# Dense 512-column matmuls added before every second key transpose job, and between the last value chunks, of a decode attention kernel

## The chip, the cores and the metric

The kernel runs on one core of one Trainium2 chip. The metric is the device time of one execution in microseconds (us). The four executions of the kernel before beside the result lie within 0.23% (448.83 to 449.87); eleven beside the experiments within 0.5 to 0.65% (447.58 to 450.48 at the widest). A single profiled execution reports a "span", from its first to its last instruction, which in these runs is 1.7 to 3.2 us shorter than the time (median 1.8). HBM is the chip's main memory, PSUM the memory that matmuls write to, in banks.

PE is the matmul engine (TensorE), PEld its weight loads, DVE the vector engine, ACT the scalar engine, POOL GpSimd, SP the engine that issues most transfers. The "granted clock" is the share of PE's full clock that the profile says was granted: in every stretch of these traces 1.00 or 0.50, and between the two only as the mean of a window with a switch in it.

## The reference, cut to what matters

Two independent decode attention blocks (one query token, batch 4, 32 query heads, 8 key/value heads, head size 128, 8192 cached positions) are computed and put side by side. Block A attends to all 8192 positions, block B to the last 2048.

```python
def _A_ref(x, k_cache, v_cache, wq, wo):          # B: the same on k_cache[:, :, Sk - W:, :]
    q = (x @ wq).reshape(B, Sq, Hq, Dh).transpose(0, 2, 1, 3)
    k = jnp.repeat(k_cache, rep, axis=1)
    v = jnp.repeat(v_cache, rep, axis=1)
    scores = jnp.einsum("bhqd,bhkd->bhqk", q, k) * (Dh ** -0.5)
    p = _softmax(scores, axis=-1)
    o = jnp.einsum("bhqk,bhkd->bhqd", p, v)
    return o.transpose(0, 2, 1, 3).reshape(B, Sq, Hq * Dh) @ wo
```

Each key and value is used by four query heads only. There is little arithmetic per byte: about 185 MB have to come in from HBM, and all of it once (184.56 MB read in the profile before).

## The kernel before

The work is cut into 40 units: 8 of block B, then 32 of block A, one for each key/value head and batch entry. A unit of block A loads 2 MB of keys and 2 MB of values. Keys arrive with positions on the partitions, so PE transposes them first: 8 jobs ("T") a unit, each of 4 transposes into a PSUM bank, which DVE (even jobs) or ACT (odd jobs) copies out. Then come score matmuls ("S", 8 columns wide), and the value matmuls ("PV", 4 columns wide) of the unit before, in four chunks of 16. PE's order within a unit is

```python
TOKENS = [("T", 0), ("T", 1), ("OT",), ("T", 2), ("T", 3), ("S", 0), ("S", 1), ("X",),
          ("T", 4), ("T", 5), ("S", 2), ("S", 3), ("PV", 0), ("PV", 1), ("OL",),
          ("T", 6), ("T", 7), ("S", 4), ("S", 5), ("PV", 2), ("PV", 3), ("S", 6), ("S", 7), ("OPJ",)]
```

OT, OL and OPJ occur in every fourth unit only (13, 17, ... 37): there the finished heads of four units are rearranged and multiplied with the output weights, four matmuls of 512 columns. The transpose job:

```python
def pe_T(u, k):
    ...
    bkf = bank_f(KTB[jobs[idx]["bank"]])
    def fn(pe):
        ins = None
        for pi in range(4):
            t0 = k * 8 + 2 * pi
            ins = pe.transpose(out=bkf[:, pi * 128:(pi + 1) * 128],
                               in_=K_sbf[:, slot, t0:t0 + 2, :].rearrange("p t d -> p (t d)"),
                               identity=identf[:, :])
        return ins
    op("pe", fn, waits=[("K", u) if k == 0 else None, bankfree(idx), ("setup",)], inc=("T", idx))
```

Keys and values each have four buffers. A key transfer is issued once the last transpose job of the unit four before it is done; a value transfer once the value work four units before is done:

```python
def sp_K(u):
    waits = [("T", tjob_idx[(u - NKS, NB - 1)])] if u >= NKS else []
    ...
def sp_V(u):
    waits = [("PV", (u - NVS) * NQ + NQ - 1)] if u >= NVS else []
    ...
```

Units 10 to 37 (LB0 to LB1 - 1) run as seven turns of a loop on PE, four units a turn, and all turns have the same instructions. Units 38 and 39 (L = 39 is the last) follow outside. Unit 38 has no value work in it; unit 39 does that of unit 37. The end of the program does what is left:

```python
for c in range(NQ):
    pe_PV(L - 1, c)
add(dve_norm(L - 1))
for c in range(NQ):
    pe_PV(L, c)
add(dve_norm(L))
pe_OPJ(L // Bn)          # the last projection: 8 matmuls of 256 columns
```

## Time and profile before

449.64 us, median of three runs (448.83 to 449.87). The profiled execution has a span of 447.8 us.

| what | value | seen in |
|---|---|---|
| DMA engines, mean busy share, 10 us windows from 20 to 430 us | 0.95 to 1.07 | windows |
| rate there from 220 us on | 421 to 432 GB/s | windows |
| PE busy | 83% | busy times |
| mean granted clock | 0.797 | cores |
| transposes of one pair of jobs (8 instructions) | 1.97 us at clock 0.50, 0.93 to 1.09 at 1.00 | timeline |

These lines of the page's 40 slices show the tenths of granted PE clock and of DMA busy share, and the rate:

```profile
PEclk9996569989886899866596689867875986788596
DMA  8999999999999999999999999999999999999991
GB/s 337 411 415 438 413 421 415 420 421 423 423 422 421 425 422 425 424 429 427 427 427 430 430 424 426 430 428 427 429 426 427 426 430 429 426 424 430 430 403 65
```

Transfers fill the program from end to end (a DMA share of 1.01 and 425 GB/s on average from 20 to 430 us) while the PE clock swings (0.50 to 1.00 in the same windows of 10 us).

PE matters where the transfers run out. Its timeline at the end of the program (start in us, duration, engine, line, operation, output <- inputs, shape, count; in brackets the idle time just before and what ended it; L332 = transposes, L371 = scores, L397 = values, L483 and L474 = projections):

```profile
411.14 1.09 PE L332 MATMUL ps<-identf,K_sb 128*128 128x128 f32 x8 [0.79 <-DMA K_sb<-in_A_k_cache_dram]
412.68 0.27 PE L416 MATMUL ps<-ident,OTg 128*16 128x128 bf16 x1 [0.44 <-DVE KT_sb L340]
413.35 1.97 PE L332 MATMUL ps<-identf,K_sb 128*128 128x128 f32 x8 [0.41 <-ACT KT_sb L341]
...
422.51 1.86 PE L483 MATMUL ps<-W,OL 128*4 128x512 bf16 x4
...
424.83 2.69 PE L332 MATMUL ps<-identf,K_sb 128*128 128x128 f32 x16
...
431.81 2.08 PE L332 MATMUL ps<-identf,K_sb 128*128 128x128 f32 x16
...
438.96 0.39 PE L397 MATMUL ps<-PT,V_sb 128*128 128x4 bf16 x10
440.17 3.31 PE L397 MATMUL ps<-PT,V_sb 128*128 128x4 bf16 x118 [0.82 <-issue]
443.79 1.86 PE L474 MATMUL ps<-W,OTg 128*4 128x256 bf16 x8 [0.31 <-DVE OTg L592]
```

The keys of unit 37 land at 411.1 us and end PE's last wait for a key transfer. From there PE is busy nearly all the time until the last projection at 443.8 (30.19 of 32.65 us). The clock falls during unit 37, from 1.00 to 0.50 at 412.71 us: the first transpose pair takes 1.09 us, the next 1.97.

### The profile page before, as it was taken

Reading aid. Unit: us, or ns where it says so; the run is one execution under the profiler, and the core shown is the slowest. Engines: PE = TensorE matmul, PEld = TensorE weight load, DVE = VectorE, ACT = ScalarE, POOL = GpSimd, SP = SyncE. Lnnn points to the kernel's source line nnn. Section 1 sums busy time; section 2 is a strip of 40 time slices with the busy share of each in tenths; the row PEclk is TensorE's granted clock in tenths of the full one; section 3 lists DMA queues with packets and bytes.
Section 4 is the critical chain, followed back from the end, with each engine's and each line's share of the span. In section 5 each row is a group of like instructions: output and inputs, shape, how many; then the busy total and the mean of one; then the engine's idle time right before and its main releaser. Section 6 shows DMA issues by size and latency. Waiting matters only on the chain.

```text
span 447.8 us, 14767 instructions
## 1 busy us (share of the span) xinstructions
PE 373.4 (83%) x6783; PEld 339.4 (76%) x6783; DVE 195.9 (44%) x451; ACT 179.2 (40%) x202; POOL 40.1 (9%) x126
## 2 busy tenths in 40 slices
PE   0685199899676999988998998899889998988997
PEld 0685199768561898878898887879878987878896
DVE  0354055656440455434363444344443544344363
ACT  1163045435330464434264434334442543435261
POOL 1100000001100011000010001000110100010010
PEclk9996569989886899866596689867875986788596
DMA  8999999999999999999999999999999999999991
GB/s 337 411 415 438 413 421 415 420 421 423 423 422 421 425 422 425 424 429 427 427 427 430 430 424 426 430 428 427 429 426 427 426 430 429 426 424 430 430 403 65
DMA packets 17270, 185.01 MB, mean 413 GB/s; under 512 B 1860, under 2 KB 2392, under 8 KB 4824
## 3 DMA queue, kind: packets, MB, share of 16 engines
q1 hardware_dynamic: 15096, 178.27, 94.4%
q10 hardware_dynamic: 2080, 6.30, 3.5%
q8 instruction: 22, 0.36, 0.3%
q14 instruction: 8, 0.07, 0.0%
q0 software_dynamic: 64, 0.01, 0.0%
HBM read 184.56 MB, written 0.01 MB: 412 GB/s over the span
## 4 chain that ended last, share of the span: by engine, by line
DMA 54%; PE 35%; issue 4%; ACT 3%; DVE 2%; POOL 0%; ACTq 0%; POOLq 0%
DMA K_sb<-in_A_k_cache_dram 41%; PE ps L332 19%; DMA W<-in_A_wq_dram 7%; DMA W<-in_B_wo_dram 6%; PE ps L397 6%; PE ps L371 5%; PE ps L483 3%; ACT KT_sb L341 3%; PE ps L278 1%; DVE KT_sb L340 1%; DVE Dt L543 0%; DVE M L505 0%; ACT PT L554 0%; PE ps L474 0%; PE ps L438 0%
## 5 line engine op out<-in xcount | busy, mean ns | idle before, releaser
L341 ACT ACTIVATE KT_sb<-ps 128x1024 bf16<-128x1024 bf16 x160 | 163.0, 1023 | 244.9 <-PE ps L332 243.1
L332 PE MATMUL ps<-identf,K_sb 128*128 128x128 f32 x1280 | 217.1, 329 | 32.9 <-DMA K_sb<-in_A_k_cache_dram 17.5
L332 PEld LDWEIGHTS ps<-identf,K_sb 128*128 128x128 f32 x1280 | 179.0, 170 | 46.2 <-DMA K_sb<-in_A_k_cache_dram 18.6
L340 DVE COPY KT_sb<-ps 128x512 int32<-128x512 int32 x160 | 110.4, 690 | 138.9 <-PE ps L332 137.7
L397 PE MATMUL ps<-PT,V_sb 128*128 128x4 bf16 (+1 forms) x2560 | 76.2, 165 | 3.6 <-DMA V_sb<-in_A_v_cache_dram 1.8
L371 PEld LDWEIGHTS ps<-RQc,KT_sb 128*128 128x128 bf16 x2048 | 72.9, 100 | 4.5 <-ACT KT_sb L341 1.2
L371 PE MATMUL ps<-RQc,KT_sb 128*128 128x8 bf16 x2048 | 74.3, 167 | 0.9 <-ACT KT_sb L341 0.8
L397 PEld LDWEIGHTS ps<-PT,V_sb 128*128 128x128 bf16 x2560 | 70.8, 97 | 3.9 <-DMA V_sb<-in_A_v_cache_dram 2.0
L575 POOL PARTITION_ALL_REDUCE LB<-L x40 | 17.3, 432 | 155.2 <-DVE L L566 155.2
L514 POOL PARTITION_ALL_REDUCE MB<-M x32 | 11.9, 371 | 173.3 <-DVE M L505 173.3
L483 PE MATMUL ps<-W,OL 128*4 128x512 bf16 x60 | 22.5, 537 | 4.8 <-DMA W<-in_B_wo_dram 4.8
L592 DVE TENSOR_TENSOR OTg<-ps,RL 128x4 bf16<-128x4 f32 (+1 forms) x40 | 6.9, 173 | 40.2 <-PE ps L397 40.2
L505 DVE TENSOR_REDUCE M<-ps 128x4 f32<-128x256 f32 (+1 forms) x40 | 19.1, 477 | 10.8 <-PE ps L371 10.8
L566 DVE TENSOR_REDUCE L<-PT 128x4 f32<-128x256 bf16 (+1 forms) x40 | 21.9, 547 | 3.3 <-ACT PT L554 2.8
L371 PE MATMUL ps<-RQB,KT_sb 128*128 128x16 bf16 x512 | 18.6, 171 | 2.1 <-issue 1.2
L371 PEld LDWEIGHTS ps<-RQB,KT_sb 128*128 128x128 bf16 x512 | 17.9, 99 | 3.0 <-issue 1.5
L554 ACT ACTIVATE PT<-Dt 128x256 bf16<-128x256 f32 (+1 forms) x40 | 18.1, 452 | 4.0 <-DVE Dt L543 2.0
L483 PEld LDWEIGHTS ps<-W,OL 128*4 128x4 bf16 x60 | 5.6, 104 | 15.3 <-issue 8.7
L278 PE MATMUL ps<-xT,W 128*128 128x4 bf16 x256 | 7.4, 165 | 10.9 <-DMA W<-in_A_wq_dram 10.6
L278 PEld LDWEIGHTS ps<-xT,W 128*128 128x128 bf16 x256 | 7.0, 101 | 11.1 <-DMA W<-in_A_wq_dram 10.7
L543 DVE TENSOR_TENSOR Dt<-ps,MB 128x256 f32<-128x256 f32 x32 | 13.3, 415 | 0.5 <-POOL MB L514 0.5
L257 PE MATMUL ps<-ident,xo_sb 4*128 4x4 bf16 x8 | 0.6, 170 | 14.2 <-POOL identf L617 14.2
(49 smaller groups left out, 64.6 us busy)
## 6 DMA issues: line engine op xcount, KB each, us to landing
K_sb<-in_A_k_cache_dram SPq DMA_DIRECT2D x32, 2048.0 KB, 32.0
V_sb<-in_A_v_cache_dram SPq DMA_DIRECT2D x31, 2048.0 KB, 36.0
K_sb<-in_B_k_cache_dram SPq DMA_DIRECT2D x16, 1024.0 KB, 28.2
V_sb<-in_B_v_cache_dram SPq DMA_DIRECT2D x16, 1024.0 KB, 28.2
W<-in_B_wq_dram SPq DMA_DIRECT2D x1, 4096.0 KB, 12.9
W<-in_A_wq_dram SPq DMA_DIRECT2D x1, 4096.0 KB, 30.0
W<-in_A_wo_dram ACTq DMA_DIRECT2D x8, 512.0 KB, 10.5
W<-in_B_wo_dram SPq DMA_DIRECT2D x1, 2048.0 KB, 29.1
```

Of the source, the lines that this page charges most:

```text
L278: ins = pe.matmul(out=bk[:, hl * Bn:(hl + 1) * Bn], lhsT=W1wq[:, c, hq * DH:(hq + 1) * DH], rhs=xT[:, P, c, :], start=(c == 0), stop=(c == ...
L332: ins = pe.transpose(out=bkf[:, pi * 128:(pi + 1) * 128], in_=K_sbf[:, slot, t0:t0 + 2, :].rearrange("p t d -> p (t d)"), identity=identf[ ...
L340: return e.tensor_copy(out=KT_sb.bitcast(I32)[:, tj % NKT, :], in_=bkf.bitcast(I32)[:, :])
L341: return e.activation(out=KT_sb[:, tj % NKT, :], in_=bk[:, :], func=ACTF.Copy)
L371: ins = pe.matmul(out=stb[:, t * CPT:(t + 2) * CPT], lhsT=ktv[:, pi, :, e], rhs=rhs, start=(e == 0), stop=(e == 1))
L397: ins = pe.matmul(out=otb[:, s * CPT:(s + 1) * CPT], lhsT=V_sb[:, vs, t, :], rhs=pt_cols(u, t * CPT, CPT), start=(j == 0), stop=(j == J - 1))
L483: ins = pe.matmul(out=opb[0:Bn, 0:D], lhsT=OL[:, i // REP, i % REP, :], rhs=wo_view[:, wg + i // REP, i % REP, :], start=(P == 1 and first ...
L505: return dve.tensor_reduce(out=M1[:, 0:NC].rearrange("p (s h) -> p s h", h=CPT), in_=stb[:, 0:NT * CPT].rearrange("p (s j h) -> p s h j", ...
L543: return dve.tensor_tensor(out=Dt[:, 0:NT * CPT].rearrange("p (s j h) -> p s j h", s=S, h=CPT), in0=stb[:, 0:NT * CPT].rearrange("p (s j h ...
L554: return act.activation(out=PT[:, u % NPT, 0:NW], in_=Dt[:, 0:NW], func=ACTF.Exp, scale=scale)
L566: return dve.tensor_reduce(out=L1[:, 0:NC].rearrange("p (s h) -> p s h", h=CPT), in_=PT[:, u % NPT, 0:NT * CPT].rearrange("p (s j h) -> p ...
L575: return pool.partition_all_reduce(LB[:, 0:NC], L1[:, 0:NC], channels=128, reduce_op=ReduceOp.add)
```

## The change

Its intent is to keep PE so dense that the granted clock stays at 1.00. In front of every second transpose job from unit 10 on, one 512-column matmul writes rubbish into the bank that the transposes then overwrite; two more go between the last unit's value chunks. No result depends on them.

```diff
+        def filler(pe, bk):
+            return pe.matmul(out=bk[:, 0:512], lhsT=ident[:, :], rhs=RQA[:, :, :, :, :].rearrange("p b g e c -> p (b g e c)"),
+                             start=True, stop=True)
+
+        def pe_filler(n):
+            idx = len(jobs) - 1
+            def fn(pe):
+                ins = None
+                for _ in range(n):
+                    ins = filler(pe, bank_f(KTB[jobs[idx]["bank"]]))
+                return ins
+            op("pe", fn, waits=[("E", idx)])
...
             def fn(pe):                        # in pe_T
                 ins = None
+                if u >= LB0 and k % 2 == 0:
+                    filler(pe, bkf)
                 for pi in range(4):
...
         for c in range(NQ):
             pe_PV(L, c)
+            if c < NQ - 1:
+                pe_filler(2)
```

That makes 112 fillers in units 10 to 37, 8 in units 38 and 39, and 6 among the last value chunks: 126.

## The prediction

> **What bounds the kernel now.** The transfers. The page's slices show the DMA engines 90% or more busy in all but the first and last, at 403 to 438 GB/s between, 185 MB in all; windows of 10 us show a DMA share of 1.00 to 1.02 up to 430 us. [...] PE is 83% busy but not the limit: in the list of waits it idles 17.5 us on A's keys, whose transfers are issued some 30 us before they land (chain of waits), so a slow PE stretch of some us starves nothing. Only the tail counts: the chain's last DMA is the key landing at 411.1 us; the end is 447.8.
>
> **What the clock does.** Windows of 1 us show only 0.50 and 1.00 in steady stretches. An 8-matmul run of transposes takes 1.97 us at 0.50 and 0.93 to 1.08 at 1.00; score runs (0.6 against 0.55) and value runs (0.99 against 0.95) hardly care. [...] the clock falls after thin score and value work (399.5, 440.2 us) and rises after 3 to 5 us of dense transposes or the 512-column projection (405.9, 426.3 us). From 413.4 to 422.5 us it stayed at 0.50 with PE busy.
>
> **What the change adds.** 512-column bf16 matmuls; from the existing ones (projection: 4 in 1.86 us at 0.50, 4 in 1.02 at 1.00) I estimate 0.43 and 0.22 us each, plus a weight load mostly hidden. Four per unit from unit 10 on: +0.9 us (warm) or +1.7 us (cold) per unit, against a unit of about 8 us warm, 11.4 cold, and a transfer time of about 10 us. Cold units get slower, but should be rarer. Six more fillers go between the last four value chunks. Nothing is removed.
>
> **On the critical path.** Steady stage: zero; a warm PE just waits longer for keys. Tail, from 411 us: three key units and three value units. If unit 37 (411 to 422) is warm it saves about 2 us net; the last value quarter lands about 440.5 us (issue 411.3 plus 29.3) and value work ends at 443.5, so at most 2.4 us can be gained. The last projection (1.86 us cold) would save 0.8 if warm. Against that, the six tail fillers cost 1.3 us warm, 2.6 cold, mostly exposed, because the value work before them lets the clock fall as before, and fillers between 0.45 us chunks are probably not dense enough to raise it. Half of 2 us gained, about 1.5 of fillers lost, 0.3 gained: near zero.
>
> **Prediction.** 449.4 us (before 449.64), 8 in 10 between 446.0 and 452.5. Faster by over 2%: 0.03; within 2%: 0.93; slower by over 2%: 0.04.
>
> **What would show it.** DMA share still 1.00 and 424 to 431 GB/s from 200 to 430 us; mean granted clock up from 0.80 to 0.85 or more; transposes' mean under 329 ns; longer PE waits on keys; the last value quarter still landing at about 440.5 us, and 6 to 9 us from there to the end, 7.3 now.
>
> **What would make it wrong.** If the fillers do not warm the clock, units cost 13 us against 10 and PE becomes the limit: 20 us or more slower. If PE's lead shortens the taper of the transfers (373 down to 147 GB/s in the last 6 us), or the tail stays warm throughout, 3 to 5 us faster.

Two passages are cut from it where marked, a ceiling for the rate of the transfers and a rule for what sets the clock. No term of its sum is among them. The sum comes to half of 2 us gained, 1.5 lost and 0.3 gained, 0.2 us lost in all ("near zero"); the figure forecast is 449.4. Two of its numbers can be read in the profile before: 512-column matmuls of the projections start 0.426 to 0.427 us apart at clock 0.50 (from 137.8 us on) and 0.215 to 0.217 at 1.00 (from 91.97 us on), which gives its 0.43 and 0.22. Its DMA share of 1.00 to 1.02 holds from 60 us on; the windows from 20 to 60 us show 0.95 to 1.07.

## The result, and the profile after

454.01 us, median of four runs (453.57 to 454.36), against 449.69 for the kernel before in the same rounds. The ratio is 1.0097, with a 95% interval of 1.0082 to 1.0111. (Ratios here are the mean time of one kernel's runs over that of the other's of the same rounds, so not quite the ratio of the medians quoted.) The change costs 1%, about 4.4 us. Its four runs had mean clocks of 0.808 to 0.845, against 0.797 in the profile before; the clock did rise a little, and the time went up.

The slices of the profiled execution after (span 452.2 us, clock 0.808):

```profile
PEclk9995555966985799998999669758955987895895
DMA  8999999999999999999999999999999999999970
GB/s 343 403 413 450 405 418 419 417 423 423 427 416 424 424 420 423 426 427 425 435 424 432 426 428 425 429 426 428 426 426 432 424 431 428 429 425 428 429 307 3
```

The transfers run as before: in windows of 1 us they carry 147 GB/s from 439 to 440 us before and 131 after, and have practically ended at 441 in both. So the transfers do not end later, and the loss is not made by holding them up in the middle. PE's timeline at the end (L319 = fillers, L348 = transposes, L413 = values, L499 and L490 = projections):

```profile
411.55 0.61 PE L319 MATMUL ps<-RQA,ident 128*128 128x512 bf16 x1 [0.90 <-DMA K_sb<-in_A_k_cache_dram]
411.95 1.91 PE L348 MATMUL ps<-identf,K_sb 128*128 128x128 f32 x8
...
423.40 1.02 PE L499 MATMUL ps<-W,OL 128*4 128x512 bf16 x4
...
425.69 0.61 PE L319 MATMUL ps<-RQA,ident 128*128 128x512 bf16 x1
...
433.89 0.38 PE L319 MATMUL ps<-RQA,ident 128*128 128x512 bf16 x1
...
441.46 1.79 PE L413 MATMUL ps<-PT,V_sb 128*128 128x4 bf16 x64
443.53 0.57 PE L413 MATMUL ps<-PT,V_sb 128*128 128x4 bf16 x16 [0.28 <-issue]
443.96 1.01 PE L319 MATMUL ps<-RQA,ident 128*128 128x512 bf16 x2
444.77 0.61 PE L413 MATMUL ps<-PT,V_sb 128*128 128x4 bf16 x16
445.24 1.01 PE L319 MATMUL ps<-RQA,ident 128*128 128x512 bf16 x2
446.05 0.61 PE L413 MATMUL ps<-PT,V_sb 128*128 128x4 bf16 x16
446.52 1.01 PE L319 MATMUL ps<-RQA,ident 128*128 128x512 bf16 x2
447.33 0.61 PE L413 MATMUL ps<-PT,V_sb 128*128 128x4 bf16 x16
448.25 1.86 PE L490 MATMUL ps<-W,OTg 128*4 128x256 bf16 x8 [0.31 <-DVE OTg L608]
```

Read the starts of corresponding pieces against each other. The columns for three of the experiments are used further below.

| start of (us) | before | after | e3 | e7 | e9 |
|---|---|---|---|---|---|
| unit 37 | 411.14 | 411.55 | 411.45 | 411.84 | 411.70 |
| its projection | 422.51 | 423.40 | 423.89 | 421.90 | 425.15 |
| unit 38 | 424.83 | 425.69 | 426.24 | 424.05 | 427.33 |
| value work of unit 38 | 438.96 | 441.46 | 440.19 | 437.44 | 441.99 |
| last projection | 443.79 | 448.25 | 444.41 | 442.11 | 446.42 |
| end of the span | 447.8 | 452.2 | 448.4 | 446.1 | 450.4 |
| clock from 412 to 418 us | 0.56 | 0.50 | 0.50 | 1.00 | 0.50 |

After against before, PE is 0.4 us late at unit 37, 0.9 at unit 38, 2.5 when the left-over value work starts, and 4.5 at the last projection. The last step is plain in the timeline. Value chunks of the last unit start 1.28 us apart (444.77, 446.05, 447.33), though a chunk without fillers takes 0.45 (64 matmuls, four chunks, in about 1.8). Two fillers thus cost 0.83, and the six 2.5; 0.5 of this is made good by a stall that only the trace before has (0.82 us idle at 440.17, against 0.28 at 443.53). And the last projection, which these fillers were meant to speed up, takes 1.86 us as it did: the clock was at 0.50 from 443 us to the end in both.

### The profile page after: what moved, and what is told of

It is laid out like the page before. It is cut to its first block, busy times and chain, and to the rows that moved or that the text cites. A ratio compares the mean times of both kernels' runs of the same rounds, so it can differ in the third digit from the quotient of the medians.

```text
span 452.2 us, 15019 instructions
## 1 busy us (share of the span) xinstructions
PE 387.0 (86%) x6909; PEld 343.1 (76%) x6909; DVE 197.5 (44%) x451; ACT 179.7 (40%) x202; POOL 40.3 (9%) x126
## 4 chain that ended last, share of the span: by engine, by line
PE 53%; DMA 39%; issue 4%; ACT 2%; DVE 1%; POOL 0%; POOLq 0%; ACTq 0%
DMA K_sb<-in_A_k_cache_dram 26%; PE ps L348 25%; PE ps L413 8%; PE ps L387 7%; DMA W<-in_A_wq_dram 7%; DMA W<-in_B_wo_dram 6%; PE ps L319 6%; PE ps L499 4%; ACT KT_sb L357 2%; PE ps L278 2%; PE ps L490 0%; PE ps L454 0%; DVE KT_sb L356 0%; DVE Dt L559 0%; DVE M L521 0%
## 5 line engine op out<-in xcount | busy, mean ns | idle before, releaser
L348 PE MATMUL ps<-identf,K_sb 128*128 128x128 f32 x1280 | 204.9, 314 | 5.2 <-DMA K_sb<-in_B_k_cache_dram 2.6
L348 PEld LDWEIGHTS ps<-identf,K_sb 128*128 128x128 f32 x1280 | 180.6, 164 | 21.7 <-issue 6.9
L413 PE MATMUL ps<-PT,V_sb 128*128 128x4 bf16 (+1 forms) x2560 | 76.8, 165 | 1.3 <-DMA V_sb<-in_A_v_cache_dram 1.1
L413 PEld LDWEIGHTS ps<-PT,V_sb 128*128 128x128 bf16 x2560 | 71.6, 97 | 3.2 <-issue 2.0
L387 PEld LDWEIGHTS ps<-RQc,KT_sb 128*128 128x128 bf16 x2048 | 69.7, 98 | 2.7 <-ACT KT_sb L357 0.9
L387 PE MATMUL ps<-RQc,KT_sb 128*128 128x8 bf16 x2048 | 71.0, 167 | 0.8 <-ACT KT_sb L357 0.8
L319 PE MATMUL ps<-RQA,ident 128*128 128x512 bf16 x126 | 56.1, 450 | 13.3 <-issue 5.3
L499 PE MATMUL ps<-W,OL 128*4 128x512 bf16 x60 | 22.2, 532 | 11.4 <-DMA W<-in_B_wo_dram 11.4
L319 PEld LDWEIGHTS ps<-RQA,ident 128*128 128x128 bf16 x126 | 12.5, 101 | 20.0 <-issue 10.3
L499 PEld LDWEIGHTS ps<-W,OL 128*4 128x4 bf16 x60 | 5.6, 105 | 22.4 <-DMA W<-in_B_wo_dram 11.5
```

Source lines behind the costliest of these rows:

```text
L319: return pe.matmul(out=bk[:, 0:512], lhsT=ident[:, :], rhs=RQA[:, :, :, :, :].rearrange("p b g e c -> p (b g e c)"), start=True, stop=True)
L348: ins = pe.transpose(out=bkf[:, pi * 128:(pi + 1) * 128], in_=K_sbf[:, slot, t0:t0 + 2, :].rearrange("p t d -> p (t d)"), identity=identf[ ...
L387: ins = pe.matmul(out=stb[:, t * CPT:(t + 2) * CPT], lhsT=ktv[:, pi, :, e], rhs=rhs, start=(e == 0), stop=(e == 1))
L413: ins = pe.matmul(out=otb[:, s * CPT:(s + 1) * CPT], lhsT=V_sb[:, vs, t, :], rhs=pt_cols(u, t * CPT, CPT), start=(j == 0), stop=(j == J - 1))
L499: ins = pe.matmul(out=opb[0:Bn, 0:D], lhsT=OL[:, i // REP, i % REP, :], rhs=wo_view[:, wg + i // REP, i % REP, :], start=(P == 1 and first ...
```

## The experiments

My theory after this reading (T in the expectations): the loss is made in the tail, behind the last key wait, by fillers that stand on PE's path, in three places (six among the value chunks, eight in units 38 and 39, four in unit 37). The rival (R): the 112 fillers of the loop make PE the limit of the long stage, buffers come free late, and the transfers end late. The first four experiments each keep a part of the change.

**e1_no_tail**: the change without the fillers among the value chunks.

```diff
             pe_PV(L, c)
-            if c < NQ - 1:
-                pe_filler(2)
```

> The change without its six fillers between the last value chunks. Theory T (the loss is made after the last large transfer has been queued: six exposed cold fillers of 0.43 us, and fillers in units 37 to 39): 454.0 minus about 2.5, so 451.5 us. Rival R (four fillers per unit make PE the limit of the steady stage, the key buffers come free late and the transfers end late): no more than 0.5 us gained, 453.5 us or more. In its trace T expects the value run of unit 39 to take 1.8 us again instead of 4.4.

Measured: 451.85 us, ratio to before 1.0046 (1.0027 to 1.0065). Half of the loss is gone with 6 of 126 fillers. In its trace the last unit's 64 value matmuls take 1.85 us again.

**e2_only_tail**: only those six.

```diff
-                if u >= LB0 and k % 2 == 0:
+                if False:
                     filler(pe, bkf)
```

> The kernel before plus only the six fillers between the last value chunks. T: plus 2.0 to 2.6 us, about 452.0 us, with the last projection still at the low clock (8 matmuls in 1.86 us). R: 449.7, as before. If these fillers warmed the clock as intended the last projection would take about 1 us.

Measured: 452.39 us, ratio 1.0055 (1.0035 to 1.0075), so 2.5 us lost (0.0055 of 449.6). The last projection takes 1.87 us, as it does at clock 0.50 in the profile before (1.86): the clock was not raised.

**e3_loop_only**: only units 10 to 37.

```diff
-                if u >= LB0 and k % 2 == 0:
+                if LB0 <= u < LB1 and k % 2 == 0:
...
-            if c < NQ - 1:
-                pe_filler(2)
```

> Fillers only in the looped units 10 to 37; none in the last two units, none between value chunks. T: only unit 37 and the key landing before it can count, plus 0.5 to 1 us: 450.5 us. R: this holds 112 of the 126 fillers, so nearly the whole loss: 453 us or more. Last keys landing and the end of the transfers within 0.5 us of the kernel before under T, 3 us later under R.

Measured: 450.98 us, ratio 1.0033 (1.0016 to 1.0051), 1.5 us lost with 112 of the 126 fillers. The start of unit 37 moves by 0.3 us only (table above), and unit 37 then runs to its projection in 12.4 us instead of 11.4, so that unit 38 starts 1.4 us late. (The profile is of the fastest of six runs, 450.44 us, and shows only 0.6 us of loss at the end, since the kernel before idles 0.82 us before its last value work, and e3 less.) The rival, which needed 453 us, falls.

**e4_last_two**: only units 38 and 39.

```diff
-                if u >= LB0 and k % 2 == 0:
+                if u >= LB1 and k % 2 == 0:
...
-            if c < NQ - 1:
-                pe_filler(2)
```

> Fillers only in units 38 and 39 (8 of 126). T: plus 1.0 to 1.7 us, 451.0 us, since both units lie after the last transfer that PE waits for and warm fillers cost up to 0.2 us each there. R: as before, 449.7 us.

Measured: 450.66 us, ratio 1.0024 (1.0007 to 1.0041), 1.1 us lost. The single profile shows less of it (span 447.9 us against 447.8), so how the 1.1 us are spread within these units stays open.

The three parts alone lose 2.5, 1.5 and 1.1 us, 5.1 together, against 4.4 for the whole change; with intervals of about 0.8 us to either side that is agreement, not a proof that they add.

The next four ask whether fillers can help where the clock matters, and what they cost elsewhere.

**e6_hold_tail**: no fillers in the units, two before each value chunk of unit 38, two after its last, and two between those of unit 39, to hold the clock up to the end.

```diff
-                if u >= LB0 and k % 2 == 0:
+                if False:
                     filler(pe, bkf)
...
         for c in range(NQ):
+            pe_filler(2)
             pe_PV(L - 1, c)
+        pe_filler(2)
         add(dve_norm(L - 1))
```

> No fillers in the units; two before and after each value chunk of units 38 and 39 (16 in all), to hold the clock up until the last projection. T: if it holds, the 16 cost about 3.5 us (0.22 each) and the projection gains 0.9: 452.2 us, so even warm the tail fillers cannot pay; if it does not hold, 16 at 0.43 us: up to 456 us. The intent of the change would want less than 449.6 us.

Measured: 452.18 us, ratio 1.0065 (1.0042 to 1.0088), 2.9 us lost; that it falls on the expected figure is luck, with six runs between 450.4 and 453.2. The clock held, 1.00 in every window to the end of the matmuls. From its timeline:

```profile
444.27 0.59 PE L319 MATMUL ps<-RQA,ident 128*128 128x512 bf16 x2
444.70 0.54 PE L413 MATMUL ps<-PT,V_sb 128*128 128x4 bf16 x16
445.10 0.59 PE L319 MATMUL ps<-RQA,ident 128*128 128x512 bf16 x2
445.53 0.54 PE L413 MATMUL ps<-PT,V_sb 128*128 128x4 bf16 x16
446.38 1.03 PE L490 MATMUL ps<-W,OTg 128*4 128x256 bf16 x8 [0.31 <-DVE OTg L608]
```

The last projection takes 1.03 us, 0.83 less. But a chunk with its two fillers takes 0.83 us instead of 0.45, so a filler costs about 0.2 us even at full clock, and the sixteen used here cost some 3 us. The sixteen kept the clock at 1.00 and did not pay: they cost more than the one thing that the clock speeds up can give. Whether fewer would hold it was not tried.

**e7_loop_double**: fillers only in units 10 to 37, but two per pair of transpose jobs.

```diff
-                if u >= LB0 and k % 2 == 0:
+                if LB0 <= u < LB1 and k % 2 == 0:
                     filler(pe, bkf)
+                    filler(pe, bkf)
...
-            if c < NQ - 1:
-                pe_filler(2)
```

> Fillers only in units 10 to 37, but two per transpose pair (224 in all). T: the transfers still bound the steady stage if a warm unit takes 8 plus 8 times 0.22 = 9.8 us against about 10; only unit 37 gets longer, by another 0.9 to 1.5 us than with one: 452 us. R (fillers in the loop cost in the steady stage): at least twice the loss of one per pair plus the stage turning PE-bound: 454 us or more, with the last keys landing over 1 us later than before.

Measured: 448.45 us, ratio 0.9983 (0.9964 to 1.0001). I had expected a further loss; twice the fillers lose nothing, and are over 2 us better than half as many (e3, ratio 1.0033). The profile says why: mean clock 0.916, and from 412 to 418 us 1.00, where it is 0.50 to 0.56 before, after and in e3. Unit 37 in e3, and then in this run:

```profile
411.45 0.61 PE L319 MATMUL ps<-RQA,ident 128*128 128x512 bf16 x1 [1.21 <-DMA K_sb<-in_A_k_cache_dram]
411.85 1.91 PE L348 MATMUL ps<-identf,K_sb 128*128 128x128 f32 x8
```

```profile
411.84 0.59 PE L319 MATMUL ps<-RQA,ident 128*128 128x512 bf16 x2
412.27 1.03 PE L349 MATMUL ps<-identf,K_sb 128*128 128x128 f32 x8
...
414.42 0.61 PE L319 MATMUL ps<-RQA,ident 128*128 128x512 bf16 x2 [0.46 <-ACT KT_sb L358]
414.86 1.04 PE L349 MATMUL ps<-identf,K_sb 128*128 128x128 f32 x8
```

Every transpose pair takes about 1.03 us, and unit 37 takes 10.1 us to its projection with eight fillers in it, against 11.4 before with none. The clock stayed up into unit 38, whose first two pairs took 2.10 us instead of 2.69.

**e5_bridge**: six fillers in front of the key wait, only in every fourth unit (13, ... 37).

```diff
-                if u >= LB0 and k % 2 == 0:
+                if False:
                     filler(pe, bkf)
...
+            def bridge(pe):
+                ins = None
+                for _ in range(6):
+                    ins = filler(pe, bkf)
+                return ins
+            if k == 0 and LB0 <= u < LB1 and u % Bn == 1:
+                op("pe", bridge, waits=[bankfree(idx)])
             op("pe", fn, waits=[("K", u) if k == 0 else None, bankfree(idx), ("setup",)], inc=("T", idx))
...
-            if c < NQ - 1:
-                pe_filler(2)
```

> The kernel before plus six fillers only in every fourth unit (13, 17, ... 37, the ones that also transpose the head outputs), put in front of the wait for that unit's keys, where PE idles 0.8 us before unit 37. T: the last key unit stays at the high clock, its three later transpose pairs take about 1.0 us instead of 1.97, so its key work ends about 3 us earlier less 0.5 us of fillers; the last value quarter (about 440.5 us) then limits the gain to 1.5 to 2.5 us: 447.5 us. If the clock in unit 37 is not on the path, or the fillers do not hold it: 449.6 to 450.5 us.

Measured: 447.82 us, ratio 0.9975 (0.9954 to 0.9996), a gain of 1.1 us, less than expected. It comes from four of six runs (447.5 to 447.9 us). The other two took 449.5 and 449.7, no less than the kernel before, and the profile is of one of these: it shows why such a run gains nothing, and where the four gained is not shown. In this profile the clock was at 1.00 for the later three transpose pairs of unit 37 (1.07 to 1.09 us each). But the six fillers themselves ran mostly at the low clock (they began at 410.90 us, and it fell at 410.96), 2.70 us in all, and kept PE past the landing of the keys (transposes from 413.39 us). Unit 38 then started 0.3 us earlier than before, and at the low clock (3.60 us for two pairs; mean clock 0.60 from 424 to 427 us).

**e8_bridge_all**: the same in each of the units 10 to 37 (the edit is shown against e5).

```diff
-            if k == 0 and LB0 <= u < LB1 and u % Bn == 1:
+            if k == 0 and LB0 <= u < LB1:
```

> As the one with six fillers ahead of the key wait, but in each of the units 10 to 37. T: same as in every fourth unit within 0.7 us, since earlier units are bound by transfers: 447.5 us if unit 37 stays warm, 450 us if not.

Measured: 456.16 us, ratio 1.0153 (1.0132 to 1.0174), 6.9 us lost. I had expected the earlier units to be free whatever they hold. They are only as long as PE can catch up. Key transfers, each issued when a unit's transposes are done, show the length of a PE-bound unit: 153.54 and 160.69 us before (7.15 us apart), 160.25 and 167.82 after (7.57), 158.22 and 166.66 in e7 (8.44), but 167.87 and 177.92 here (10.05):

```profile
153.54 0.34 SPq L648 DMA_DIRECT2D K_sb<-in_A_k_cache_dram  x1
160.69 0.33 SPq L648 DMA_DIRECT2D K_sb<-in_A_k_cache_dram  x1
...
167.87 0.33 SPq L671 DMA_DIRECT2D K_sb<-in_A_k_cache_dram  x1
177.92 0.33 SPq L671 DMA_DIRECT2D K_sb<-in_A_k_cache_dram  x1
```

(The first two lines are of the kernel before, the last two of e8.) Transfers take about 10.1 us a unit (in the kernel before, units 33 and 37 start on their keys' landing at 370.72 and 411.14 us, 40.4 us for four). PE falls behind while it waits for the output weights of block B, which land at 137.4 us before and 139.6 in e8, and in e8, at 10.0 us a unit (27 units from 148.74 us on), it never makes that up: the first filler of unit 37 starts at 418.5 us, where that unit starts at 411.1 to 411.8 in the runs of the table. The transfers still carried 424 to 434 GB/s from 220 to 430 us, but for one window of 421, and had ended by about 440, so even here they were not held up; the whole lag was paid at the end.

The last two ask which fillers of e7 hold the clock in unit 37.

**e9_ot_double**: two per pair in units 13, 17, ... 37 only (the edits of the last two are shown against e7).

```diff
-                if LB0 <= u < LB1 and k % 2 == 0:
+                if LB0 <= u < LB1 and u % Bn == 1 and k % 2 == 0:
```

> Two fillers per transpose pair, but only in every fourth unit (13, 17, ... 37). If what gained in the run with two per pair in all looped units (448.4 us) was the high clock in unit 37 alone, and the fillers of unit 37 alone can raise it: 448.5 us and transposes of unit 37 at about 1.0 us per pair. If the clock has to be held through the key wait by the units before: unit 37 starts at the low clock with cold fillers (8 at 0.43) and the run is 450 to 452 us.

Measured: 451.85 us, ratio 1.0046 (1.0027 to 1.0066). The timeline at unit 37:

```profile
409.34 0.54 PE L388 MATMUL ps<-RQc,KT_sb 128*128 128x8 bf16 x16
411.70 0.64 PE L319 MATMUL ps<-RQA,ident 128*128 128x512 bf16 x1 [1.81 <-DMA K_sb<-in_A_k_cache_dram]
412.12 1.91 PE L349 MATMUL ps<-identf,K_sb 128*128 128x128 f32 x8
...
415.15 1.03 PE L319 MATMUL ps<-RQA,ident 128*128 128x512 bf16 x2 [0.83 <-ACT KT_sb L358]
415.98 1.91 PE L349 MATMUL ps<-identf,K_sb 128*128 128x128 f32 x8
```

PE was ahead, idled 1.81 us, and the clock fell before the first filler of unit 37 came (at 410.45 us, 0.6 us into the idle time). Eight fillers, six of them at half clock (the last two, at 422.38 us, took 0.38 us at full), then made unit 37 take 13.5 us to its projection.

**e10_two_double**: two per pair in units 36 and 37, and each such pair of units before.

```diff
-                if LB0 <= u < LB1 and k % 2 == 0:
+                if LB0 <= u < LB1 and u % Bn < 2 and k % 2 == 0:
```

> As before it, with two fillers per pair in units 36 and 37 and every such pair of units (12, 13, 16, 17, ...), none in the other two. If the unit ahead of the key wait is what holds the clock: unit 37 at the high clock and 448.4 us as with two per pair everywhere. If not: as with unit 37 alone.

Measured: 448.96 us, ratio 0.9996 (0.9975 to 1.0018), 2.9 us better than e9. The clock was at 1.00 from 409 to 439 us and unit 37 at the high clock throughout. So between these two runs the fillers of the unit ahead of the key wait decide whether unit 37 starts at the high clock; fillers in unit 37 alone did not bring it there (0.50 from 412 to 418 us in e9). e9 and e10 do not tell apart whether PE must be dense there or must not idle, since the fillers of unit 36 also let PE arrive late, with no wait for keys.

The kept traces tell more; the following was worked out from them afterwards. In all twelve, every stretch at one clock, but for the first and last, measures a whole multiple of 3.413 us (before, the switches at 399.06, 405.89, 412.71, 426.37 and 440.02 us lie 2, 2, 4 and 4 times that apart). So one can count, in each of these windows, the columns that PE streams: 512 for a filler, 256 for a transpose, because eight transposes take as long at full clock (0.87 us) as four fillers (0.86 us, e7), and for a score and a value matmul their 8 and 4 columns times 1.2, a factor chosen in counting (with 1.0 the traces before and after divide as cleanly, 3372 at most against 3456 at least); a matmul across an edge counts whole in both windows. From 150 us on, in the traces before and after, there are 173 such windows: each with 3480 columns or more was followed by one at full clock, each with fewer by one at half. If transposes are left out, no limit gets fewer than 66 of the 173 wrong, so in these traces they count. With the limit of 3480 left as it is, 832 of the 854 windows of the other ten traces come out right; the time that PE was busy, with its own best limit from the first two traces, gives 679. Two windows from e5 and e7 (us from the span's start, length, PE busy with count, PEld, DVE, ACT, POOL; then clock, DMA share, GB/s) show how little idle time says:

```profile
407.55:410.96 3.41, 3.41 (x112) 3.40 (x110) 0.86 (x2) 1.85 (x2) 0.00 (x0) 1.00 1.04 442
...
412.38:415.79 3.41, 2.51 (x23) 1.94 (x22) 2.06 (x5) 1.33 (x2) 0.37 (x1) 1.00 1.01 432
```

In the first (e5, ahead of unit 37) PE never idled, but 2.4 us of it went to the narrow scores and values, it streamed only 3241 columns, and the clock fell at 410.96 us. In the second (e7) PE idled 0.9 us, streamed 5788 columns, and the clock stayed. This also fits the dose. A unit has 8960 columns without fillers, 11008 with four and 13056 with eight. Spread over the 10.1 us of its transfers, that is an estimated 3030, 3720 and 4410 a window. These are to be set against about 3130, the limit when each matmul of the two traces is spread over its time instead of counted whole at the edges: too few, enough on average, and enough with room. With four, the thin end of unit 36 fell short: the window before the clock fell held 3379 columns in the profile after and 3020 in e3.

The windows lie differently against the program in each execution, so one trace is one draw. Before, e2, e4 and e6 have the same code up to unit 38, and their first transpose pair of unit 37 took 1.09, 1.09, 1.74 and 1.97 us. The comparison of e3 and e7 does not hang on one draw: the clock from 412 to 418 us was 0.50 to 0.59 in all four of these, 0.50 in all three profiles with one filler per pair (after, e1, e3), and 1.00 in both with two through unit 36 (e7, e10).

No version beats the kernel before by more than 0.3%; e5's interval just excludes 1, and e7's does not. In e7 PE begins the left-over value work at 437.4 us, with value transfers still landing until about 440, so probably little more can be had from PE's side; this was not tested.

## Why the prediction was wrong

The range, 446.0 to 452.5 us, missed 454.01. The class (within 2%) was right.

- *The transfers bound the kernel and the steady stage costs nothing*: right for the change. Rate and end of the transfers are unchanged, and e3 moves unit 37 by 0.3 us. e8 shows its limit: it holds as long as a unit takes PE less than the roughly 10 us of its transfers.
- *Cost of a filler*: 0.43 and 0.22 us predicted, 0.42 (0.83 for two, after) and about 0.2 (e6) measured. In the units a filler at full clock costs at most 0.1 us: in the one pair of units compared, unit length grows from 7.15 to 7.57 us with four of them (in the next pair from 7.52 to 7.59), so the predicted 0.9 us per unit was at least twice too much.
- *The tail sum* is the step that failed: "Half of 2 us gained, about 1.5 of fillers lost, 0.3 gained: near zero."
  - The half chance of 2 us for unit 37 was a loss. Its clock stayed low (0.50 from 412 to 418 us), and the loop's fillers cost 1.5 us (e3). One filler per pair did not hold the clock through the key wait (0.50 from 412 to 418 us in after, e1 and e3); two through unit 36 did (1.00 in e7 and e10).
  - Fillers in units 38 and 39 were not in the sum at all. They lie behind the last key wait just as unit 37 does, and cost 1.1 us (e4).
  - The six tail fillers cost 2.5 us (e2), not about 1.5: all of them ran at the low clock (1.01 us for two) and none was hidden. With them, PE streamed 2340 columns in the window from 442.50 us, under the 3480 that the other windows show it takes.
  - The projection gained nothing: 1.86 us before and after.
- *The mean clock rises to 0.85 or more*: not reached, 0.808 to 0.845. *Transposes under 329 ns*: yes, 314. *Longer PE waits on keys*: no. In the list of waits, A's keys cost PE 17.5 us before and 3.2 after. PE with its fillers is later, not earlier, although its clock is higher.
- *6 to 9 us from the last value landing to the end*: it is about 11.7 (452.2 less the 440.5 of the prediction, from where the transfers hardly moved).

The traces show only 0.50 and 1.00 away from the switches, and the switches lie whole multiples of 3.413 us apart. In the kernel before the last ones come at 399.06, 405.89, 412.71, 426.37 and 440.02 us (the prediction's 399.5 and 440.2 are a little late). What the prediction did not do is judge each window of the tail, filler by filler; "more dense" was not enough where a window fell short (3379 columns before the clock fell in the profile after).

## What to carry to other kernels

This is one kernel; what it showed is this. While transfers bounded it, PE work in the middle was free as long as PE caught up before the last transfers landed (112 fillers moved the start of unit 37 by 0.3 us in e3; in e8, at 10.0 us a unit, PE did not catch up and 6.9 us were lost). What stood behind its last wait was paid (2.5 us for the six fillers of e2, 1.1 for the eight of e4), so add up every added instruction there, in each stage, before hoping for a faster clock. Filler pays only if the work that it speeds up and that lies on the path is longer than the filler itself; in the tail here 0.8 us could be won for some 3 us of filler. To judge whether the clock will hold, count the columns streamed in each window, not the time that PE is busy (832 against 679 of 854 windows right here). A filler that fell short of holding the clock was charged at the low clock, 0.42 us instead of about 0.2, and half a dose was worse than none and worse than a double dose (ratios 1.0033 in e3, 0.9983 in e7).
